# Threshold attention and a squared-ReLU layer on one core: the attention part's steps put in new orders, with values and turned weights in other PSUM banks

## The chip, the core and the metric

One NeuronCore of a Trainium2 chip runs the whole program. TensorE (PE) multiplies matrices and transposes; its weight loader is listed apart as PEld. VectorE (DVE), ScalarE (ACT) and GpSimd (POOL) do the elementwise work, and SyncE's queue (SP) issues nearly all DMAs. The metric is the device time of one execution in microseconds (us); the median of three runs stands for a kernel.

## What is computed

The reference runs attention in which only scores close to each row's maximum count, and feeds the result to a two-layer network:

```python
# q, k, v: (8, 8, 576, 64) float32; tau = 0.02
scores = q @ k.transpose(0, 1, 3, 2) / 8
thresh = scores.max(-1, keepdims=True) - tau
scores = where(scores >= thresh, scores, -1e9)
attn = exp(scores - scores.max(-1, keepdims=True))
attn = attn / (attn.sum(-1, keepdims=True) + 1e-9)
x = (attn @ v).transpose(0, 2, 1, 3).reshape(4608, 512)
out = maximum(x @ w_in, 0) ** 2 @ w_out      # w_in (512, 2048), w_out (2048, 512)
```

The two weight matrices arrive as 64-bit floats and are turned into 32-bit ones on the chip.

## The kernel before

The program has two parts, one after the other. The attention part comes first. The feed-forward part (`hidden_layer`, L837, and `output_layer`, L955) then does two layers of products with a seven-product scheme of sums and differences applied twice; its matmuls are L849 and L984. The change leaves it as it is.

**Units and periods.** A pair `i` is two heads of one batch entry, 32 in all. A unit is a block of 128 queries of both heads of a pair; every ninth unit (in two pairs) is made of the two rests of 64 queries. There are 144 units, handled two at a time (A and B) in 72 periods `p`. `period(p)` (L624) walks through a written list of step names and calls each; every engine executes its own steps in that order. Three lists exist: `PLAIN` (L599), `CONVERTING` (L602) for periods in which a chunk of the weights is also converted (`converts`, L590, periods 2 to 34), and `FIRSTS` (L606) for periods 0, 1 and 2.

**The steps** of one pair of units, in the order in which the data needs them:

- `T` turns (transposes) queries or keys of a later pair on PE into the middle of PSUM banks 1 and 4 (L399); `eT` evicts them with ACT (L406, L414) and issues the loads of the pair after that. `load_k` (L301) and `load_q` (L291) put these on SP's queue.
- `SA`: PE computes the main scores of A (banks 0 and 5) and the 64 last columns of A and B (the rims of banks 1 and 4); `SB`: the main scores of B (banks 2 and 3). Line L438.
- `topA0` to `topB1`: DVE copies a block of scores out of PSUM and takes its extreme (L456). `least`: POOL adds tau to it (L463). `pow`: ACT's exponential (L466). `mask`: DVE zeroes what is beyond the threshold and sums each row (L471).
- `over` (POOL, L478), `inv` (DVE, L481) and `spread` (POOL, L521) make the reciprocals of the row sums and write them out wide.
- `V`, `W`, `U`: PE turns the weights of 8, 2 (and the wide reciprocals) and 8 blocks (`half_turn`, L377, the transposes of L381); `eV`, `eW`, `eU`: ACT copies them to SBUF (`filled`, L523, the copies of L528).
- `PV`: PE multiplies by the values (`values`, L530, the matmuls of L537). `x`: DVE scales one head's result out of PSUM (L658), ACT copies the other's (L660). `xs`: POOL scales that one (L675) and SP stores both (L585).
- `c1` to `c6`: conversion of a chunk of weights: two passes on ACT (c1 L205, c2 L211), two on DVE (c4 L226, c5 L234), two on POOL (c3 L218, c6 L245). In the second half of the chunks a store follows c6 on SP's queue. `fetch` loads a chunk. `s1` and `sV` do one sum of weights on POOL, four on DVE (L122, L125). `id4`, `id14` keep PE busy in the first periods.

**PSUM before.** Eight banks of 512 columns. Six belong to the tile `sc`: banks 0 and 5 take A's main scores and later PV's result, banks 2 and 3 take B's main scores and later W (`middle`, L621), banks 1 and 4 the rims and T. The other two banks are the tile `pt`, one buffer, used in turn by U and by V. In period `p` the lists work on units of different ages: U, PV, x of the units of period `p - 2`, V, W, over, inv, spread of `p - 1`, scores to masks of `p`.

**Waits.** The framework makes an instruction wait for those whose data or buffers it needs. For the tile `sc`, `touch` (L356) sets this by bank: it adds a wait between two engines that touch the same bank and takes away one between different banks, except for the pairs of kinds in `MEET` (L354), which also meet in SBUF.

## Time and profile before

| what | us |
|---|---|
| median of three runs | 1290.56 |
| lowest and highest | 1289.38, 1292.22 |
| the profiled execution | 1292.2 |
| its span, first to last instruction | 1290.4 |
| busy in the span: PE, its loader | 1261.3, 1127.2 |
| busy in the span: DVE, POOL, ACT | 998.5, 897.4, 854.9 |
| mean granted clock of TensorE | 0.999 |

The span is the time between the first and the last instruction; some 1.8 us lie around it. Busy times of an engine are unions of its instructions' intervals, and an instruction of ACT or DVE is listed with its whole latency, so the next one often begins before the last has ended: what an engine can do is read from start to start. In a row of a timeline or of the chain stand the start, the duration, the engine, the line, the operation or the tile that it writes, and the count of instructions merged in it; in brackets the idle time ahead of it and what ended that. `sc` and `pt` are the PSUM tiles, `arena` is SBUF.

### The profile page before, as it was taken

How to read it: one execution, taken by the hardware profiler on the slowest of the kernel's cores; microseconds unless marked ns; L12 is line 12 of the kernel's file. 1: busy time of each engine (PE TensorE's matmuls, PEld its weight loads, DVE VectorE, ACT ScalarE, POOL GpSimd, SP SyncE). 2: the span in 40 equal slices, each digit the busy share in tenths (PEclk: the TensorE clock that was granted, in tenths of full speed). 3: DMA queues.
4: the chain of work that ended last, by engine and by line, in shares of the span. 5: the costliest groups of instructions: out<-in, count | busy, mean ns of one | idle time of the engine just before them, and what ended most of it. 6: DMA issues, size and time to landing. Idle time of an engine off the chain costs nothing.

```text
span 1290.4 us, 46352 instructions
## 1 busy us (share of the span) xinstructions
PE 1261.3 (98%) x18627; PEld 1127.2 (87%) x18627; DVE 998.5 (77%) x2433; ACT 854.9 (66%) x1536; POOL 897.4 (70%) x1094
## 2 busy tenths in 40 slices
PE   8999998999999999999999999999999999999998
PEld 6666666677777768999999999999999999999998
DVE  6999999899999997787788778777745654665463
ACT  6999999899999995756675667566523432343240
POOL 2565565555555557888898789768777867776775
PEclk9999999999999999999999999999999999999999
DMA  5555666544333422556655665589545314522411
GB/s 149 157 149 152 162 189 182 140 94 115 88 83 83 103 48 67 180 169 205 204 185 177 212 199 178 176 322 394 188 148 164 113 57 160 165 90 79 160 34 34
DMA packets 247032, 192.05 MB, mean 149 GB/s; under 512 B 97184, under 2 KB 195488, under 8 KB 246816
## 3 DMA queue, kind: packets, MB, share of 16 engines
q1 hardware_dynamic: 245360, 188.63, 48.7%
q8 instruction: 147, 2.41, 0.8%
q10 hardware_dynamic: 1456, 0.44, 0.1%
q14 instruction: 69, 0.57, 0.1%
HBM read 116.65 MB, written 72.35 MB: 146 GB/s over the span
## 4 chain that ended last, share of the span: by engine, by line
PE 64%; DMA 2%; DVE 1%; ACT 1%; issue 0%; POOL 0%; SPq 0%; ACTq 0%; DVEq 0%; POOLq 0%
PE ph L849 30%; PE po L984 29%; PE sc L537 2%; PE sc L438 2%; DMA wall<-w 1%; PE pt L381 1%; DMA g<-arena 0%; PE sc L381 0%; PE sc L399 0%; DVE arena L456 0%; ACT c L795 0%; ACT arena L528 0%; DVE arena L125 0%; DVE arena L122 0%; POOL arena L125 0%
## 5 line engine op out<-in xcount | busy, mean ns | idle before, releaser
L125 POOL TENSOR_TENSOR arena<-arena 128x512 f32<-128x512 f32 (+1 forms) x314 | 378.1, 1224 | 108.7 <-DVE arena L125 92.0
L984 PE MATMUL po<-wall,arena 128*128 128x128 f32 x3528 | 394.7, 275 | 1.4 <-ACT arena L761 1.4
L984 PEld LDWEIGHTS po<-wall,arena 128*128 128x128 f32 x3528 | 394.3, 192 | 1.8 <-ACT arena L761 1.8
L849 PE MATMUL ph<-arena,wall 128*128 128x128 f32 x3528 | 394.4, 275 | 0.5 <-DVE arena L658 0.5
L849 PEld LDWEIGHTS ph<-arena,wall 128*128 128x128 f32 x3528 | 394.1, 192 | 0.7 <-ACT arena L660 0.6
L125 DVE TENSOR_TENSOR arena<-ph,arena 128x512 f32<-128x512 f32 x378 | 256.1, 688 | 86.9 <-PE ph L849 62.6
L122 POOL TENSOR_TENSOR arena<-arena 128x128 f32<-128x128 f32 (+2 forms) x314 | 255.2, 814 | 54.5 <-DMA arena<-w 36.7
L125 DVE TENSOR_TENSOR arena<-po,arena 128x128 f32<-128x128 f32 x378 | 108.2, 289 | 168.4 <-PE po L984 164.3
L466 ACT ACTIVATE arena<-arena 128x576 f32<-128x576 f32 x288 | 224.3, 858 | 16.7 <-DVE arena L456 16.7
L471 DVE SCALAR_TENSOR_TENSOR arena<-arena 128x576 f32<-128x576 f32 x288 | 225.7, 812 | 0.4 <-POOL arena L463 0.3
L456 DVE TENSOR_SCALAR_CACHE_REDUCE arena<-sc 128x576 f32<-128x576 f32 x288 | 204.2, 750 | 18.0 <-ACT arena L528 6.8
L795 ACT COPY c<-arena 128x512 f32<-128x512 f32 (+1 forms) x303 | 173.5, 579 | 49.5 <-DVE arena L122 41.5
L537 PEld LDWEIGHTS sc<-arena 64*64 64x64 f32 x5760 | 144.8, 133 | 44.3 <-DVE arena L456 40.4
L122 DVE TENSOR_TENSOR arena<-arena,c 128x512 f32<-128x512 f32 (+1 forms) x267 | 174.6, 662 | 5.8 <-ACT c L795 4.0
L438 PE MATMUL sc<-arena 64*64 64x64 f32 (+1 forms) x2304 | 170.6, 417 | 0.3 <-DVE arena L658 0.2
L537 PE MATMUL sc<-arena 64*64 64x128 f32 (+1 forms) x5760 | 160.6, 262 | 9.9 <-DVE arena L456 7.8
L528 ACT COPY arena<-pt 128x1024 f32<-128x1024 f32 x144 | 157.4, 1093 | 3.6 <-PE pt L381 3.6
L761 ACT COPY arena<-po 128x128 f32<-128x128 f32 x63 | 16.6, 264 | 186.8 <-PE po L984 184.0
L381 PEld LDWEIGHTS pt<-ident,arena 64*128 64x128 f32 x2304 | 83.3, 139 | 42.7 <-ACT arena L528 35.3
L761 ACT COPY arena<-ph 128x512 f32<-128x512 f32 x63 | 36.6, 581 | 121.8 <-PE ph L849 121.2
L381 PE MATMUL pt<-ident,arena 64*128 64x64 f32 x2304 | 101.0, 228 | 3.7 <-ACT arena L528 3.5
L438 PEld LDWEIGHTS sc<-arena 64*64 64x64 f32 x2304 | 62.8, 133 | 47.0 <-issue 22.6
(51 smaller groups left out, 941.4 us busy)
## 6 DMA issues: line engine op xcount, KB each, us to landing
g<-arena SPq DMA_DIRECT2D x144, 256.0 KB, 2.8
arena<-g SPq DMA_DIRECT2D x144, 256.0 KB, 4.2
w<-arena SPq DMA_DIRECT2D x60, 256.0 KB, 2.5
wall<-w SPq DMA_DIRECT2D x49, 256.0 KB, 5.3
arena<-w SPq DMA_DIRECT2D x44, 256.0 KB, 3.1
arena<-in_v_dram SPq DMA_DIRECT2D x32, 288.0 KB, 3.6
out_dram<-arena SPq DMA_DIRECT2D x70, 128.0 KB, 2.5
arena<-in_q_dram SPq DMA_DIRECT2D x64, 128.0 KB, 3.8
```

What stands on the lines that cost most here:

```text
L122: e.tensor_tensor(out=out, in0=x, in1=y, op=ALU.subtract)
L125: e.tensor_tensor(out=out, in0=x, in1=y, op=ALU.add)
L381: made = nc.tensor.transpose(pt[:, r, ts(slot, HALF)], of[rows, :], ident[rows, rows])
L438: made = nc.tensor.matmul(sc[at, ds(to, count)], lhs, kT[rows, ds(at_k, count)], start=True, stop=True)
L456: made = nc.vector.tensor_scalar(out=s[:, j, :], in0=sc[:, ds(at, S)], scalar1=1.0, scalar2=None, op0=ALU.mult, op1=ALU.min, accum_out=nmx ...
L466: nc.scalar.activation(out=w[:, :, j, :], in_=of(j), func=AF.Exp, bias=nmx[:, j : j + 1], scale=-1.0)
L471: nc.vector.scalar_tensor_tensor(out=w[:, :, j, :], in0=of(j), scalar=thr[:, j : j + 1], in1=w[:, :, j, :], op0=ALU.is_le, op1=ALU.mult, a ...
L528: touch("weights", nc.scalar.copy(joined(to), whole(pt, 0, count)), at, 2 * BANK, m)
L537: made = nc.tensor.matmul(sc[ds(u * D, D), ds(5 * j * BANK + row, count)], loaded_v[i][rows, (c - (u != j)) % CH, :], wT[m][rows, ds(weigh ...
L795: nc.scalar.copy(c, y)
L849: nc.tensor.matmul(to[:, j, :], W_IN[m, k][:, ts(j, P)], of[k][:, m - 1, :], start=(not more and j == 0), stop=True, skip_group_check=True,)
L984: nc.tensor.matmul(to, g[:, j, :], w[:, j, :], start=(not more and j == 0), stop=(j == 3), skip_group_check=True)
```

## The change

- PV's result goes to the tile `pt`, which it shares with U. V moves to `middle` (banks 2 and 3), W to banks 0 and 5. W is evicted by two copies, one a bank. `MEET` loses two kinds of pairs that no longer meet in `sc`.
- All lists are new. A step name may carry a lag (`leastA@1`, `eV@2`): `period(p)` then does that step for the units of period `p - lag`. `LAGS` has the default lags. When the lists change from one period to the next, `due` sees that each step is done once for every period.
- In `PLAIN`, least, mask and one power of a period move to the start of the next; V's and W's evictions lag into the next period; T, U stand ahead of the scores, PV right behind them, W and V at the end.
- In `CONVERTING`, U moves one period earlier, between SA and SB; T moves from the start to behind W; c5 and c6 from the end to the start; c3 and c4 to the same period as c1.
- `converts` is true for one period more (2 to 35), and there is a list for period 3.
- `load_k` loads the last key rows of both heads by one DMA and not by two, and evictions of T go in the other order of banks.

```diff
-            queue.dma_start(out=rn[REST:P, ds(j * D, D)], in_=keys[:, CH - 1, :])
         queue = nc.sync if i else nc.scalar
-        queue.dma_start(
-            out=rn[0:REST, :].rearrange("p (j d) -> p j d", j=2),
-            in_=q[b, h : h + 2, MAIN:S, :].rearrange("j p d -> p j d"),
-        )
+        both = lambda rows: rn[rows, :].rearrange("p (j d) -> p j d", j=2)
+        last = k[b, h : h + 2, :, :].rearrange("j (p c) d -> p c j d", c=CH)[:, CH - 1, :, :]
+        nc.sync.dma_start(out=both(ds(REST, REST)), in_=last)
+        queue.dma_start(out=both(ds(0, REST)), in_=q[b, h : h + 2, MAIN:S, :].rearrange("j p d -> p j d"))
...
-    MEET = (("q scores", "turned q", (Q_RING,)), ("scores", "turned k", (K_RING,)), ("q scores", "turned k", (K_RING,)), ("values", "weights", (W_RING,)), ("x", "weights", (W_RING,)))
+    MEET = (("q scores", "turned q", (Q_RING,)), ("scores", "turned k", (K_RING,)), ("q scores", "turned k", (K_RING,)))
...
-                for r, n in ((0, half), (1, half + REST)):
+                for r, n in ((1, half + REST), (0, half)):
...
-                for r in range(2):
+                for r in (1, 0):
...
-        to = wT[m][:, ds(weight_at(first) * P, count * P)]
-        touch("weights", nc.scalar.copy(joined(to), whole(pt, 0, count)), at, 2 * BANK, m)
-
-    def values(m):
+        to = joined(wT[m][:, ds(weight_at(first) * P, count * P)])
+        if f == "W":
+            for r in (1, 0):
+                of = pt[r][:, ds(0, count * HALF)].rearrange("p (t q) -> p t q", q=HALF)
+                touch("weights", nc.scalar.copy(to[:, r, :, :], of), at[r], BANK, m)
+            return
+        of = pt[:, :, ds(0, count * HALF)].rearrange("p r (t q) -> p r t q", q=HALF)
+        touch("weights", nc.scalar.copy(to, of), at, 2 * BANK, m)
+
+    def values(m, to):
...
-                        made = nc.tensor.matmul(
-                            sc[ds(u * D, D), ds(5 * j * BANK + row, count)], loaded_v[i][rows, (c - (u != j)) % CH, :],
+                        nc.tensor.matmul(
+                            to[ds(u * D, D), j, ds(row, count)], loaded_v[i][rows, (c - (u != j)) % CH, :],
...
-        return is_wide and (has_chunk(p) or has_chunk(p - 1))
+        return is_wide and any(has_chunk(p - i) for i in range(3))
...
     PLAIN = """
-        fetch U SA topA1 over s1 topA0 SB topB1 inv sV eU powA1 V topB0 leastA spread PV powA0 maskA1 leastB maskA0 eV T powB1 x maskB1 powB0 xs maskB0 eT W eW
+        fetch leastA@1 eW@2 U leastB@1 maskA0@1 maskB0@1 maskA1@1 powB1@1 maskB1@1 eV@2 T SA topA0 over inv sV s1 eU eT xs@3 SB topA1 spread topB0 powA0 PV topB1 powA1 powB0 W x V
     """.split()
     CONVERTING = """
-        fetch c1 T SA topA1 c3 topA0 U eU powA1 SB topB0 over topB1 powA0 c4 powB0 PV eT inv leastA maskA1 x powB1 leastB spread V eV maskA0 W maskB0 c5 c6 eW maskB1 xs c2
+        fetch over SA c5 eV@2 c1 c6 topA1 U@1 topA0 leastA eU@1 powA1 inv SB xs@3 PV powA0 spread topB0 maskA1 W powB0 topB1 maskA0 T c3@0 c2 powB1 eW x c4@0 leastB maskB1 V eT maskB0
     """.split()

     FIRSTS = {
         0: """
-            SA SB id4 fetch topA1 topA0 powA1 leastA powA0 topB1 T id14 powB1 topB0 powB0 eT maskA0 leastB maskA1 maskB1 maskB0
+            fetch U@1 SA W spread topA1 SB topA0 powA1 eU@1 leastA topB0 powA0 topB1 powB1 maskA0 powB0 V eW leastB maskA1 id14 T x maskB1 eT PV xs@3 id4 maskB0 over eV@2 inv
         """.split(),
         1: """
-            SA topA1 SB topA0 id4 topB0 over inv powA1 V eV spread T powA0 topB1 eT W id4 leastA maskA1 leastB powB1 maskA0 maskB1 powB0 maskB0 fetch eW
+            fetch over SA topA1 id4 powA1 SB inv topA0 powA0 topB0 powB0 topB1 leastA spread leastB U@1 maskA1 W eW maskB0 eV@2 T powB1 eT PV eU@1 maskB1 maskA0 x xs@3 V
         """.split(),
         2: """
-            T SA fetch c2 U topA1 c3 over eU SB powA1 topA0 c4 powA0 c5 topB0 powB0 leastA topB1 eT maskA1 PV inv powB1 V leastB x spread maskA0 eV maskB1 maskB0 W eW xs c6 c1
+            fetch SA eV@2 over topA1 c5 c1 inv topA0 U@1 leastA c6 eU@1 powA1 SB PV powA0 spread topB0 W powB0 maskA1 xs@3 c2 topB1 maskA0 T c3@0 powB1 c4@0 leastB eW V maskB0 eT x maskB1
+        """.split(),
+        3: """
+            fetch c5 eV@2 c1 over SA U@1 topA1 c6 topA0 leastA xs@3 inv eU@1 SB topB0 spread PV powA1 topB1 W c2 powA0 maskA1 powB0 T c3@0 c4@0 leastB powB1 eW maskB0 eT x V maskB1 maskA0
         """.split(),
     }

+    LAGS = dict(
+        U=2, V=1, W=1, eU=2, eV=1, eW=1, PV=2, x=2, xs=2, over=1, inv=1, spread=1, c3=1, c4=1, c5=1, c6=1,
+    )
+    due, late = {}, {}
...
+    def turned_weights(f, m):
+
+        if not has(2 * m):
+            return
+        if f == "U":
+            late[f, m] = pt_pool.tile([P, 2, BANK], FP32, tag="pt", name="pt")
+            fill(m, f, [late[f, m][:, r, :] for r in range(2)])
+        elif f == "V":
+            late[f, m] = middle()
+            fill(m, f, [late[f, m][:, r, :] for r in range(2)], (2 * BANK, 3 * BANK))
+        else:
+            late[f, m] = [sc[:, ds(b * BANK, BANK)] for b in (0, 5)]
+            fill(m, f, late[f, m], (0, 5 * BANK))
+
+    def evict(f, m):
+
+        if has(2 * m):
+            filled(m, f, late.pop((f, m)), {"U": None, "V": 2 * BANK, "W": (0, 5 * BANK)}[f])
...
+    def values_of(m):
+
+        if has(2 * m):
+            late["PV", m] = pt_pool.tile([P, 2, BANK], FP32, tag="pt", name="px")
+            values(m, late["PV", m])
+
+    def given_out(m):
+
+        if not has(2 * m):
+            return
+        of = late.pop(("PV", m))
+        x = sb.tile([P, 2, P], FP32, tag="x", bufs=2, name="x")
+        one = nc.vector.tensor_tensor(out=x[:, 0, :], in0=of[:, 0, 0:P], in1=wT[m][:, ts(SCALE_AT, P)], op=ALU.mult)
+        other = nc.scalar.copy(x[:, 1, :], of[:, 1, 0:P])
+        tc.declare_no_dep(other.ins, one.ins, reason="other halves")
+        late["x", m] = x, wT.pop(m)
+        valued(m)
...
+    def period(p):
+
+        todo = []
+        for at, step in enumerate(FIRSTS.get(p) or (CONVERTING if converts(p) else PLAIN)):
+            name, _, lag = step.partition("@")
+            if name in in_order:
+                todo.append((p, at, in_order[name], p))
+                continue
+            lag = int(lag or LAGS.get(name, 0))
+            for q in range(due.get(name, 0), p - lag + 1):
+                todo.append((q + lag, at, steps[name], q))
+            due[name] = max(due.get(name, 0), p - lag + 1)
+        for _, _, step, q in sorted(todo, key=lambda t: t[0:2]):
+            step(q)
```

140 lines of the change are left out of this document (48 added, 92 removed).

## Prediction

> **What bounds it now.** I read the table by stages first (busy time in windows cut at the first score matmul of periods 0, 3, 36 and 71 and at the first matmul of the feed-forward part), then the chain that ended last, then the timelines of single periods. Columns of the table: window, its length, then busy time (instructions) of PE, PEld, DVE, ACT, POOL, the granted clock, DMA share and GB/s.
>
> ```profile
> 8.32:27.51 19.19, 17.11 (x295) 11.21 (x294) 16.49 (x48) 13.93 (x25) 4.50 (x10) 1.00 0.65 174
> 27.51:262.32 234.81, 218.93 (x5287) 154.96 (x5284) 228.26 (x659) 230.32 (x403) 140.03 (x231) 0.99 0.59 159
> 262.32:481.79 219.47, 218.38 (x5592) 158.01 (x5590) 211.07 (x631) 209.27 (x355) 121.47 (x210) 1.00 0.38 87
> 481.79:496.19 14.40, 11.96 (x364) 9.67 (x365) 13.32 (x33) 9.89 (x16) 5.38 (x11) 1.00 0.16 31
> 496.19:1290.41 794.22, 788.92 (x7056) 788.25 (x7056) 528.62 (x1062) 388.68 (x735) 625.36 (x628) 1.00 0.50 164
> ```
>
> The last row, 794.22 us, is the feed-forward part with PE and its loader full; the change doesn't touch it. What can move is the 487.9 us above it: 33 converting periods (7.12 us each), where ACT and DVE are both 97 to 98% busy and PE is not the bound, and 35 plain ones (6.27 us each), where PE has 1.1 us to spare in 219. In a plain period the chain is PE from end to end:
>
> ```profile
> 435.16 2.19 PE sc L537 x72
> 437.36 0.45 PE sc L399 x10
> 437.81 0.25 PE sc L381 x8
> 438.06 0.50 PE pt L381 x16
> 438.56 2.26 PE sc L438 x32
> 440.82 0.65 PE pt L381 x16
> ```
>
> That is PV, T, W, U, the scores SA and SB, and V: 6.30 us. The rows to look at are the 16 transposes: 0.50 behind other transposes, 0.65 behind scores. A change of matmul form costs about 0.15 in the piece behind it, and there are four a period (into T, into scores, into V, into PV).
>
> **Plain periods, part by part.** New PE order: U T | SA SB PV | W V, and on into U. V now stands behind W (0.50 for 0.65), W pays the form change that T paid (T: 0.45 less 0.14, W: 0.25 plus 0.14, nothing in sum), PV stands behind scores and not behind transposes; that saving has no row of its own, so 0 to 0.2, and I take 0.15 like the others. PE's work: 6.30 - 0.15 - 0.15 = 6.00 with ten T transposes (bounds 5.95 to 6.15), less with eight or none. PE falls to where DVE already is:
>
> ```profile
> 438.86 0.81 DVE L471 SCALAR_TENSOR_TENSOR arena<-arena 128x576 f32<-128x576 f32 x1
> 439.60 0.08 DVE L471 DVE_READ_ACCUMULATOR arena<-arena 128x1 f32 x1
> 439.95 0.76 DVE L456 TENSOR_SCALAR_CACHE_REDUCE arena<-sc 128x576 f32<-128x576 f32 x1 [0.28 <-ACT arena L528]
> ...
> 477.19 0.76 DVE L456 TENSOR_SCALAR_CACHE_REDUCE arena<-sc 128x576 f32<-128x576 f32 x1
> ...
> 483.18 0.76 DVE L456 TENSOR_SCALAR_CACHE_REDUCE arena<-sc 128x576 f32<-128x576 f32 x1
> ```
>
> From 477.19 to 483.18, the same step of two periods without a T, DVE never pauses: 5.99 us is its own period. At 439.95 it has waited 0.28, for PE's scores by the order of the steps (the row names ACT, whose copy it doesn't read). So of 6.27 at most 0.28 can go. A mask takes 0.74 (438.86 to 439.60), four are 2.96, and the other 3.03 are tops, inverse and x.
>
> The new order makes a ring of DVE and POOL that the old one did not have. The masks of a period run in the next one, ahead of its tops; leastA, which the first mask needs, stands on POOL behind over, s1, xs and spread, and over needs the last mask of the period before. The POOL rows:
>
> ```profile
> 439.77 0.23 POOL L478 TENSOR_SCALAR arena<-arena 128x4 f32<-128x4 f32 x1 [1.46 <-DVE arena L471]
> 440.08 1.28 POOL L122 TENSOR_TENSOR wall<-wall 128x512 f32<-128x512 f32 x1
> 441.50 0.29 POOL L463 TENSOR_SCALAR arena<-arena,tau_p 128x2 f32<-128x2 f32 x1
> 442.30 0.40 POOL L521 COPY arena<-arena 128x256 f32<-128x256 f32 x1 [0.51 <-DVE arena L481]
> 442.91 0.79 POOL L463 TENSOR_SCALAR arena<-arena,tau_p 128x2 f32<-128x2 f32 x1 [0.22 <-DMA arena<-in_k_dram]
> 444.20 0.46 POOL L675 TENSOR_TENSOR arena<-arena 128x128 f32<-128x128 f32 x1 [0.50 <-ACT arena L660]
> ```
>
> Last mask's end (439.60 + 0.08) to over 0.09, over to s1 0.31, s1 1.28, xs 0.46, spread 0.40, leastA 0.29: 2.83, and 3.1 with a gap like the one after over (0.08) at each hand-over. DVE's own work from the same point is 3.03 - 0.08 = 2.95. So the first mask comes 0 to 0.15 late. leastB comes right behind leastA and so beside the first mask; the second L463 row, which ran beside masks, took 0.79 against 0.29. The second mask (0.74 after the first) then waits about 0.1, or 0.3 (its own 0.29) if leastB only gets through when the mask ends. Together 5.99 to 6.45. I take 6.12: 0.05 for the late leastA and 0.1 for leastB (0.79 plus a hand-over, less 0.74, the nearest row).
>
> The Trainium skill, SBUF - State Buffer, section Who interferes with whom, says that a DVE instruction with two SBUF inputs contends with a GpSimd instruction that reads SBUF, and that the later one blocks. The mask has two such inputs, and 0.79 against 0.29 agrees; by that rule leastB would be held to the mask's end every period, the upper end of the last paragraph.
>
> PV's result now shares its buffer with U, and U must wait until x has been read by DVE and, behind powB0, by ACT. This ring: first top 0.75, the end of T's eviction 0.4, three powers 2.01 (row below), x and its hand-over 0.45, U 0.5, T 0.3, form change 0.15, SA to the first top 1.3: 5.9, hidden behind DVE's 5.99 and gone as cover from 0.1 on. ACT's own work (four powers 2.68, two wide copies 1.78, W 0.52, T 0.8, x 0.15, by the rows below) is 5.9 too. The first plain period inherits no U and no masks; I put it at 5.85. So plain: 5.85 + 34 x 6.12 = 213.9, **5.5 less**.
>
> **Converting periods.** ACT and DVE set them:
>
> ```profile
> 162.05 0.98 ACT L211 ACTIVATE arena<-arena 128x512 int32<-128x512 uint32 x1
> 162.64 0.95 ACT L205 ACTIVATE arena<-arena 128x512 f32<-128x512 f32 x1
> 163.23 1.27 ACT L528 COPY arena<-pt 128x1024 f32<-128x1024 f32 x1
> 164.12 2.38 ACT L466 ACTIVATE arena<-arena 128x576 f32<-128x576 f32 x3
> 166.13 0.96 ACT L414 COPY arena<-sc 128x256 f32<-128x256 f32 x2
> 166.70 0.60 ACT L406 ACTIVATE arena<-sc,qscale 128x64 f32<-128x64 f32 x1
> ```
>
> ACT is in line from start to start: c2 0.59, a 1024-wide copy 0.89, three powers 2.01. DVE's own period there is 6.9 (228.26 / 33 busy). Nothing of this work goes away. W's one eviction becomes two of half the width: the two key copies took 0.57 (166.13 to 166.70, of 256 and 320), so about 0.52 for the 0.48 of one, 0.04 more. And the order ties a ring: SA, U, eU, powA1, powA0, powB0, c2, powB1, eW, and SA again, because W now lies in SA's own banks and U stands between SA and SB.
>
> ```profile
> 160.72 1.32 PE L438 MATMUL sc<-arena 64*64 64x512 f32 x24
> 162.00 0.71 PE L381 MATMUL pt<-ident,arena 64*128 64x64 f32 x16
> ```
>
> SA to U 1.28, U 0.71, hand-over 0.1, eU 0.89, powers 2.01, c2 0.59, powB1 0.67, eW's first copy 0.26 and its second with the hand-over 0.45: 6.96, say 7.0. A period with a T or k eviction has ACT work of 7.0 to 7.1 (now 7.02 to 7.12). I take 7.08 for 31 periods, and 6.5 for the two that convert nothing but keep the order: 232.5, **2.3 less**. The gain is not in the order itself but in two places where the present order loses:
>
> ```profile
> 223.90 0.43 PE L399 MATMUL sc<-ident,arena 64*128 64x64 f32 x7 [0.36 <-DMA arena<-in_k_dram]
> 225.41 0.34 PE L399 MATMUL sc<-ident,arena 64*128 64x64 f32 x2 [1.08 <-DMA arena<-in_q_dram]
> ...
> 255.48 0.71 PE L381 MATMUL pt<-ident,arena 64*128 64x64 f32 x16 [1.35 <-ACT arena L528]
> ```
>
> In the first two T waits for its rows; the third is the seam to the plain order. Without these 2.8 us the present periods are (234.81 - 2.8) / 33 = 7.03. T moves from the period's start to behind PV; c6, whose store stands on SP's queue ahead of the loads, moves from the period's end to its start, so loads leave most of a period earlier against their T; two key DMAs become one. I count these losses gone, and nothing for fetch, c1 to c6 and the stores: they lie beside ACT's queue. If that cover is gone, a T late by a load costs 1 to 1.5 us each time.
>
> **Ends.** Start: DVE waits for T's form in banks 1 and 4 twice, as here:
>
> ```profile
> 12.33 0.76 DVE L456 TENSOR_SCALAR_CACHE_REDUCE arena<-sc 128x576 f32<-128x576 f32 x1 [0.50 <-PE sc L399]
> ...
> 489.64 2.06 DVE L122 TENSOR_TENSOR wall<-wall 128x512 f32<-128x512 f32 x3
> ```
>
> T now follows the tops in periods 0 and 1: **1.0 less** for two such waits. Tail, from the last SA: to the first top 1.45, tops and x 3.05, the masks held over 3.1, over and inverse 0.7, four sums of the last row's kind 2.7, x 0.4, U 0.6, eU 1.1, PV 2.7 (it is one with a rest block), x 0.5: 16.3 for the 14.40 of now, **1.9 more**. One POOL sum (1.28) moves into the feed-forward part; 0 to 1.3, taken as 0, since POOL has 169 us free there.
>
> Sum: -5.5 - 2.3 - 1.0 + 1.9 = -6.9. The profiled run took 1292.2 (span 1290.4 and 1.8 around it), so 1285.3; it lay 1.6 above the median of the three runs, so **1283.7** as a median.
>
> **Rivals.** (1) **Both rings close at their floors**: plain 5.99, converting 7.0: 209.5 and 230, with the ends' +0.9 in all -13.9: 1276.7. For it: DVE did run at 5.99. Against: two rings of POOL and ACT with no slack. (2) **ACT's ring in the converting periods is longer than its parts**: 0.08 more at each of four hand-overs makes 7.3, 31 x 0.22 = 6.8 back: 1290.5, no change. (3) **Slower**: leastB is held behind the first mask in every plain period and leastA is late too: 6.45 x 34 + 5.85 = 225.2, 5.7 more than now; with the other terms +4.3: 1294.9. Slower by over 0.2% it is from a plain period of 6.40 on. For it: 0.79 beside masks; against: leastB may get in before the mask, since the mask waits for leastA anyway.
>
> **How the numbers follow.** A measurement of this kernel can tell about 0.2% (2.6 us) from no change. Forecast 0.55, rival 1 0.15, rival 2 0.12, rival 3 0.18. Faster 0.70, same 0.12, slower 0.18. The likeliest case by itself spans 1279 to 1288 (plain 5.99 to 6.22); the range goes down to rival 1 and up to the foot of rival 3: 1275 to 1293.
>
> **What would show it.** Plain periods of 6.0 to 6.2 with DVE without gaps but one small one ahead of the first or second mask, released by POOL; the 16 transposes of V at 0.50; converting periods of 7.0 to 7.1 with no PE wait on loads; a tail of 16. Wrong if plain periods stay over 6.3, if PE waits for x ahead of U, or if SA waits on eW for more than 0.2.

## The result, and the profile after

The changed kernel took **1296.2 us** (median of 6, 1294.2 to 1296.7), the kernel before 1290.1 beside it: a ratio of 1.0043 with an interval of 1.003 to 1.0056. In a later set beside other runs of the kernel before the ratio was 1.0019 (1.0001 to 1.0036). It is 0.2 to 0.4% **slower**; the forecast was 1283.7, faster, and the time lies above the range's end of 1293.

This is the table by stages of the changed kernel's profile (window, its length, then busy time and instructions of PE, PEld, DVE, ACT, POOL, the granted clock, DMA share, GB/s), cut at the same places as the one in the prediction:

```profile
8.04:27.28 19.24, 16.71 (x301) 10.58 (x300) 16.89 (x48) 15.05 (x27) 5.26 (x11) 1.00 0.77 201
27.28:266.11 238.83, 215.27 (x5288) 147.91 (x5288) 233.92 (x662) 233.32 (x438) 150.03 (x229) 1.00 0.57 155
266.11:481.34 215.23, 213.69 (x5582) 158.30 (x5581) 209.91 (x625) 206.90 (x387) 118.41 (x209) 1.00 0.38 87
481.34:499.58 18.24, 13.65 (x367) 11.23 (x365) 14.59 (x35) 10.74 (x18) 6.00 (x11) 0.91 0.16 30
499.58:1294.82 795.24, 789.05 (x7056) 788.29 (x7056) 528.62 (x1062) 388.53 (x735) 626.63 (x629) 1.00 0.50 164
```

| stage | before, us | after, us | change | forecast |
|---|---|---|---|---|
| up to the first scores | 8.32 | 8.04 | -0.3 | 0 |
| periods 0 to 2 | 19.19 | 19.24 | 0 | -1.0 |
| converting, 33 periods | 234.81 | 238.83 | +4.0 | -2.3 |
| plain, 35 periods | 219.47 | 215.23 | -4.2 | -5.5 |
| last scores to feed-forward | 14.40 | 18.24 | +3.8 | +1.9 |
| feed-forward | 794.22 | 795.24 | +1.0 | 0 |

The changes add up to the spans' 4.4. The plain periods gained nearly what was worked out. The converting stage and the tail took it back, and more. One caution on the column "before": two later profiles of that kernel have 232.2 and 231.4 in the converting stage, so its first profile, on which the forecast rests, carried some 3 us there that are not usual. Against these two the converting stage lost 7 us and not 4.

**Plain periods.** 6.27 us became 6.16 (34 periods from period 37 on). DVE's and POOL's rows around one hand-over in the timeline (L466 is the mask, L458 least) show what is left above DVE's own time:

```profile
436.76 0.91 POOL L458 TENSOR_SCALAR arena<-arena,tau_p 128x2 f32<-128x2 f32 x1
436.78 0.81 DVE L466 SCALAR_TENSOR_TENSOR arena<-arena 128x576 f32<-128x576 f32 x1
437.52 0.08 DVE L466 DVE_READ_ACCUMULATOR arena<-arena 128x1 f32 x1
437.70 0.82 DVE L466 SCALAR_TENSOR_TENSOR arena<-arena 128x576 f32<-128x576 f32 x1
```

leastB starts beside the first mask and ends at 437.67, just behind the mask's end (437.60); the second mask, of B, starts at 437.70, 0.10 late. All later steps follow without a pause.

**Converting periods.** ACT's rows of one period, from eV to the next eV, in the timeline:

```profile
165.55 1.04 ACT L529 COPY arena<-sc 128x1024 f32<-128x1024 f32 x1
166.44 0.72 ACT L205 ACTIVATE arena<-arena 128x512 f32<-128x512 f32 x1
167.03 1.04 ACT L529 COPY arena<-pt 128x1024 f32<-128x1024 f32 x1
167.93 2.14 ACT L461 ACTIVATE arena<-arena 128x576 f32<-128x576 f32 x3
169.93 0.74 ACT L211 ACTIVATE arena<-arena 128x512 int32<-128x512 uint32 x1
170.52 0.81 ACT L461 ACTIVATE arena<-arena 128x576 f32<-128x576 f32 x1
171.19 0.68 ACT L526 COPY arena<-sc 128x256 f32<-128x256 f32 x2
171.71 0.33 ACT L672 COPY arena<-px 128x128 f32<-128x128 f32 x1
171.86 0.77 ACT L409 COPY arena<-sc 128x320 f32<-128x320 f32 x2
172.44 0.40 ACT L401 ACTIVATE arena<-sc,qscale 128x64 f32<-128x64 f32 x1
172.65 1.10 ACT L529 COPY arena<-sc 128x1024 f32<-128x1024 f32 x1
```

No row has idle time ahead of it: 7.10 us from eV to eV is ACT's own work. PE waits in such a period, at SA for eW (next fence), but it waits for an engine that is not idle.

```profile
164.83 1.37 PE L433 MATMUL sc<-arena 64*64 64x512 f32 x24 [0.38 <-ACT arena L526]
```

The prediction named a wait of SA for eW of more than 0.2 as a sign of being wrong. It came, but by itself it doesn't tell a ring that sets the period from slack. Beside the periods around a stop of PE (below) and one wait of 0.3 in period 4, ACT runs dry only in the three places where no T is evicted, and then for U:

```profile
115.96 0.71 ACT L205 ACTIVATE arena<-arena 128x512 f32<-128x512 f32 x1
117.22 1.01 ACT L529 COPY arena<-pt 128x1024 f32<-128x1024 f32 x1 [0.55 <-PE pt L380]
```

Of the 31 periods that convert, 28 took 7.11 on average (forecast 7.08). Three single ones (4, 6 and 29) took 7.57, 9.14 and 7.77, and the two that convert nothing (34 and 35) 6.79 and 8.45 where 6.5 each was forecast. The 9.14 is a stop of PE in the middle of 16 transposes; the bracket gives the idle time and "issue", which is to say that nothing the profile shows was waited for:

```profile
55.28 0.54 PE L380 MATMUL sc<-ident,arena 64*128 64x64 f32 x11
57.94 0.34 PE L380 MATMUL sc<-ident,arena 64*128 64x64 f32 x5 [2.12 <-issue]
```

The 8.45 is the seam to the plain order. There T stands ahead of SA, and it writes where eT of the period before, the last step of ACT in the converting list, still reads; DVE then has nothing to do:

```profile
264.62 0.86 ACT L401 ACTIVATE arena<-sc,qscale 128x256 f32<-128x256 f32 x2
...
265.54 0.59 PE L394 MATMUL sc<-ident,arena 64*128 64x64 f32 x10 [1.30 <-ACT arena L401]
...
267.50 0.76 DVE L451 TENSOR_SCALAR_CACHE_REDUCE arena<-sc 128x576 f32<-128x576 f32 x1 [1.77 <-issue]
```

**Tail.** PE stands still until eU, last in ACT's queue, is done. PV then takes 3.77 for 72 matmuls, which took 2.19 in the fence of the prediction (435.16):

```profile
489.76 3.77 PE L538 MATMUL px<-arena 64*64 64x128 f32 x72 [2.23 <-ACT arena L529]
...
496.61 2.33 PE L538 MATMUL px<-arena 64*64 64x128 f32 x108 [1.65 <-ACT arena L529]
```

The reason why it took longer stands in the clock's column (the 0.54 and 0.60) of the table by windows:

```profile
488.00:490.00 2.00, 0.24 (x8) 0.25 (x12) 1.65 (x7) 1.70 (x2) 0.23 (x1) 1.00 0.01 1
490.00:492.00 2.00, 2.00 (x48) 2.00 (x44) 1.93 (x4) 0.00 (x0) 1.20 (x2) 0.54 0.11 22
492.00:494.00 2.00, 2.00 (x47) 1.67 (x42) 1.57 (x4) 0.27 (x1) 0.08 (x1) 0.60 0.27 52
```

DVE is not what the tail waits for. It stands idle ahead of its last step, x of the last pair, until PV is done:

```profile
499.14 0.29 DVE L671 TENSOR_TENSOR arena<-px,arena 128x128 f32<-128x128 f32 x1 [2.48 <-issue]
```

### The profile page after: what moved, and what is told of

It is laid out like the page before. It is cut to its first block, busy times and chain, and to the rows that moved or that the text cites. A ratio compares the mean times of both kernels' runs of the same rounds, so it can differ in the third digit from the quotient of the medians.

```text
span 1294.8 us, 46358 instructions
## 1 busy us (share of the span) xinstructions
PE 1254.4 (97%) x18623; PEld 1121.4 (87%) x18623; DVE 1004.6 (78%) x2433; ACT 857.5 (66%) x1608; POOL 907.0 (70%) x1094
## 4 chain that ended last, share of the span: by engine, by line
PE 67%; ACT 14%; issue 5%; DVE 5%; DMA 4%; POOL 2%; SPq 2%; ACTq 0%; DVEq 0%; POOLq 0%
PE ph L865 30%; PE po L1000 27%; ACT arena L529 4%; ACT arena L461 4%; PE sc L433 4%; PE px L538 3%; DVE arena L451 2%; DVE arena L466 2%; PE sc L380 1%; ACT arena L526 1%; PE pt L380 1%; POOL arena L458 1%; ACT arena L401 1%; SPq L310 1%; DMA arena<-g 1%
## 5 line engine op out<-in xcount | busy, mean ns | idle before, releaser
L466 DVE SCALAR_TENSOR_TENSOR arena<-arena 128x576 f32<-128x576 f32 x288 | 229.0, 824 | 5.5 <-POOL arena L681 0.3
L461 ACT ACTIVATE arena<-arena 128x576 f32<-128x576 f32 x288 | 211.8, 798 | 9.0 <-DVE arena L451 8.9
L451 DVE TENSOR_SCALAR_CACHE_REDUCE arena<-sc 128x576 f32<-128x576 f32 x288 | 207.0, 746 | 7.9 <-PE sc L433 4.5
L538 PEld LDWEIGHTS px<-arena 64*64 64x64 f32 x5760 | 146.1, 134 | 66.7 <-ACT arena L529 65.8
L538 PE MATMUL px<-arena 64*64 64x128 f32 (+1 forms) x5760 | 162.1, 263 | 11.4 <-ACT arena L529 10.1
L473 POOL TENSOR_SCALAR arena<-arena 128x4 f32<-128x4 f32 x72 | 28.7, 399 | 161.1 <-DVE arena L466 157.2
L433 PEld LDWEIGHTS sc<-arena 64*64 64x64 f32 x2304 | 56.6, 132 | 71.1 <-issue 23.7
L458 POOL TENSOR_SCALAR arena<-arena,tau_p 128x2 f32<-128x2 f32 x144 | 80.0, 556 | 39.5 <-DVE arena L451 27.1
L845 ACT ACTIVATE arena<-arena 128x512 f32<-128x512 f32 x144 | 90.8, 631 | 4.6
```

The lines of the kernel that those rows point to most:

```text
L433: made = nc.tensor.matmul(sc[at, ds(to, count)], lhs, kT[rows, ds(at_k, count)], start=True, stop=True)
L451: made = nc.vector.tensor_scalar(out=s[:, j, :], in0=sc[:, ds(at, S)], scalar1=1.0, scalar2=None, op0=ALU.mult, op1=ALU.min, accum_out=nmx ...
L458: nc.gpsimd.tensor_scalar(out=thr, in0=nmx, scalar1=tau_p[:, :], scalar2=None, op0=ALU.add)
L461: nc.scalar.activation(out=w[:, :, j, :], in_=of(j), func=AF.Exp, bias=nmx[:, j : j + 1], scale=-1.0)
L466: nc.vector.scalar_tensor_tensor(out=w[:, :, j, :], in0=of(j), scalar=thr[:, j : j + 1], in1=w[:, :, j, :], op0=ALU.is_le, op1=ALU.mult, a ...
L538: nc.tensor.matmul(to[ds(u * D, D), j, ds(row, count)], loaded_v[i][rows, (c - (u != j)) % CH, :], wT[m][rows, ds(weight_at(2 * c + u) * P ...
```

## The experiments

My theory after this profile was that W, now in the banks of SA's scores, ties ACT and PE into a ring that sets the converting periods, and that the tail lost to a halved clock. The rivals were: ACT's own work sets the periods; single stalls and the seam cost what was lost; the new PSUM places rather than the orders are at fault. Ratios are to the kernel before, run beside each; the changed kernel's own are 1.0043 and 1.0019.

**One step off the supposed ring.**

```diff
-... T c3@0 c2 powB1 eW x c4@0 leastB ...      (CONVERTING)
+... T c3@0 powB1 eW c2 x c4@0 leastB ...
```

> Only the order of the converting periods is changed: the conversion step c2 (0.59 us on ACT) is issued behind eW and not ahead of powB1. Theory: the 31 converting periods of 7.1 to 7.2 us are a ring through ACT and PE (SA, U, eU, powA1, powA0, powB0, c2, powB1, eW, SA), because W now lies in the banks of SA's scores; with c2 off the ring PE no longer waits for eW ahead of SA, and a period falls to ACT's own work of about 7.0: 0.1 to 0.15 x 31, 3 to 5 us less than the changed kernel's 1296.2, so 1291.5 to 1293. Rival (the periods are ACT's own work, and the ring only shows a wait that costs nothing): the wait moves to eU, periods stay 7.12 to 7.16, 1295.5 to 1297. Rival (the loss is stalls of single periods, such as the 9.14 us of period 6): typical periods as before this edit, the long ones still there.

Ratio **1.0128** (1.011 to 1.0146), 1308.0 us: some 12 slower than the changed kernel, which neither theory nor rivals had. Periods are 7.5 to 7.6 with a T of keys or queries, 6.87 without. ACT's rows:

```profile
159.15 2.16 ACT L461 ACTIVATE arena<-arena 128x576 f32<-128x576 f32 x3
161.66 0.78 ACT L461 ACTIVATE arena<-arena 128x576 f32<-128x576 f32 x1 [0.34 <-DVE arena L451]
162.34 0.62 ACT L526 COPY arena<-sc 128x256 f32<-128x256 f32 x2
162.85 0.70 ACT L211 ACTIVATE arena<-arena 128x512 int32<-128x512 uint32 x1
```

powB1 needs DVE's fourth top, which comes 0.34 after the third power's end; c2 had filled just that gap. And eT, which SA's last columns need, still stands behind c2. A step that "sits on a chain" was the filler of a wait. That ACT idles here in every period, and the period grows, speaks for ACT as the bound.

**U at the head of the period.**

```diff
-fetch over SA c5 eV@2 c1 c6 topA1 U@1 topA0 ...      (CONVERTING)
+fetch over U@1 SA c5 eV@2 c1 c6 topA1 topA0 ...
```

> Only the order of the converting periods is changed: U is issued at the head of the period, ahead of SA and not behind it, so that eU need not follow SA. Theory of the ring: SA to U (1.28 us) falls out of it, no wait of PE on eW of more than 0.1 is left, and the periods fall to ACT's work: 7.0 or a little under, 31 x 0.15 = 4 to 5 us less than the changed kernel: 1291 to 1292.5. Rival (ACT's own work): 7.12 to 7.16 as in the changed kernel, 1295.5 to 1297. A second way to go wrong: SA starts 0.7 later behind U, and DVE's first tops with it; if DVE (6.9 us a period) then becomes late, the periods are 7.2 to 7.4 and the time 1298 to 1303.

Ratio **1.0562** (1.054 to 1.0584), 66 to 70 us slower, periods of 8.5 to 9.9. I had overlooked what U reads:

```profile
164.79 0.28 PE L380 MATMUL pt<-ident,arena 64*128 64x64 f32 x2 [0.55 <-ACT arena L672]
166.07 0.71 PE L380 MATMUL pt<-ident,arena 64*128 64x64 f32 x14 [1.00 <-DVE arena L466]
```

U turns the weights of the period before, whose last mask is DVE's last step; ahead of SA it makes masks, U, SA and tops one chain with nothing of DVE's beside it. So this run doesn't tell the ring from ACT's work. It shows why U stands behind SA.

**Masks in the order A A B B.**

```diff
-... maskA0@1 maskB0@1 maskA1@1 powB1@1 maskB1@1 eV@2 T SA ...      (PLAIN)
+... maskA0@1 maskA1@1 maskB0@1 powB1@1 maskB1@1 eV@2 T SA ...
```

> Only the order of the plain periods is changed: both masks of A come ahead of those of B, so that the second mask no longer needs leastB, which POOL makes beside the first. Theory: the 0.10 to 0.18 us of DVE's idle time ahead of the second mask is all that is left above DVE's own 5.99; plain periods fall from 6.15 to 6.0 to 6.05, 34 x 0.1 to 0.15: 3.5 to 5 us less than the changed kernel, 1291 to 1293. Rival (leastA is late as well, or PE's and ACT's ring through x, U and eU is as long): the idle time moves to the first mask or to the tops, periods 6.12 to 6.18, 1295 to 1297.

Ratio **1.0014** (1.0001 to 1.0027), 1292.9 us: 2.4 to 3.4 less than the changed kernel. Plain periods fell from 6.16 to 6.08 and the stage from 215.23 to 212.55. DVE's rows:

```profile
435.45 0.81 DVE L466 SCALAR_TENSOR_TENSOR arena<-arena 128x576 f32<-128x576 f32 x1
436.19 0.08 DVE L466 DVE_READ_ACCUMULATOR arena<-arena 128x1 f32 x1
436.19 0.81 DVE L466 SCALAR_TENSOR_TENSOR arena<-arena 128x576 f32<-128x576 f32 x1
...
438.72 0.76 DVE L451 TENSOR_SCALAR_CACHE_REDUCE arena<-sc 128x576 f32<-128x576 f32 x1 [0.19 <-ACT arena L401]
```

The second mask now starts when the first ends. Part of the gain goes to a new wait: the masks end earlier, and the second top waits. In this profile the tail took 19.70, 1.5 more, with the clock halved twice in it and not once. Half theory, half rival.

**PE kept busy in the tail.** Sixteen transposes of the identity ahead of PV in period 72.

```diff
+    in_order["idT"] = lambda p: p == NU // 2 and keep_busy(16, sc[:, ds(BANK, P)])
-... topB0 powA0 PV topB1 powA1 powB0 W x V      (PLAIN)
+... topB0 powA0 idT PV topB1 powA1 powB0 W x V
```

> One step is added in the period behind the last scores alone: 16 transposes of the identity, which write to a bank that nobody reads, ahead of PV. Theory: in the tail PE stood still for 2.23 us for eU, the granted clock then was 0.5 for 3.4 us, and PV took 3.77 for the 2.20 that it takes elsewhere; with PE at work during the wait the clock stays at 1.0, PV takes 2.2 to 2.4, and the tail from the last SA to the feed-forward part falls from 18.24 to about 16.7: 1294.7. Rival (the 0.5 is not an answer to the idle time, or PV is slow for another reason): 18.2 as before, or the transposes themselves run at half speed and PV still takes over 3: 1296 to 1297.

Ratio 1.004 (1.0026 to 1.0054), no different from the changed kernel. The mechanism is there: the clock stays at 1.00, and

```profile
487.44 1.04 ACT L529 COPY arena<-pt 128x1024 f32<-128x1024 f32 x1
487.62 1.97 PE L1053 MATMUL sc<-ident 128*128 128x128 f32 x16 [1.31 <-ACT arena L529]
...
489.51 2.20 PE L538 MATMUL px<-arena 64*64 64x128 f32 x72
```

PV takes 2.20, 1.57 less. But the tail is 17.61, only 0.6 shorter: the sixteen transposes outlast the wait that they fill. eU (the ACT row) ends at 488.48 and PV starts 1.03 behind it, where it started 0.06 behind it in the changed kernel.

**A period of its own for the seam.**

```diff
-        return is_wide and any(has_chunk(p - i) for i in range(3))
+        return is_wide and any(has_chunk(p - i) for i in range(2))
+        35: fetch leastA@1 eW@2 U leastB@1 maskA0@1 maskB0@1 maskA1@1 powB1@1 maskB1@1 eV@2 SA topA0 over
+            inv s1 eU xs@3 SB topA1 spread topB0 powA0 PV topB1 T powA1 powB0 W eT x V      (FIRSTS)
```

> The converting order ends one period earlier (after period 34), and period 35 has a list of its own, the plain order with T behind SB and eT behind W. In the changed kernel the last two periods before the plain stage took 6.79 and 8.45 us: the second because T(36) stands ahead of SA in the plain order and waited 1.30 us for eT(35) at the end of the converting one, with DVE idle for 1.77. Theory (a seam between the two orders, a term the forecast had at zero): the two periods become 6.2 to 6.6 each, 2 to 2.8 us less in that stage, 1293.4 to 1294.2 in all against the changed kernel's 1296.2. Rival (the 1.30 us is slack, ACT and DVE have the same work anyway): the time moves into the neighbouring periods and the sum of periods 34 to 37 stays within 0.5 us, 1296.

Ratio 1.0031 (1.0016 to 1.0046). Periods 34 and 35 took 7.28 and 7.38, 14.66 for the 15.24 of the changed kernel's first profile: 0.6 less, not 2 to 2.8. PE's 1.30 was mostly slack of two orders that hand over work of different ages; the price of this seam is 0.6 as far as this list can take it away.

**The old list on the new places.** The converting list of the kernel before, all else as changed.

> The list of the converting periods is that of the kernel before, while values and turned weights keep their new PSUM places; lists of the first four periods, the plain one and all else are the changed kernel's. It tells places from orders. Theory 1 (ACT's and DVE's work sets the period, and neither place nor order matters much): typical periods of 7.0 to 7.1, 1293 to 1297. Theory 2 (W in the banks of SA's scores needs the new order): SA must wait for eW, which stands at the end of the old list, so SA, four tops, c4, two masks, W and eW are one chain: 1.45 + 2.7 + 0.6 + 0.1 + 0.73 + 0.2 + 0.73 + 0.25 + 0.5 + hand-overs is 7.4 to 7.6 a period, 31 x 0.35 to 0.45 is 11 to 14 us more than the changed kernel: 1307 to 1310.

Ratio **1.0316** (1.0292 to 1.034), periods of 8.13 to 8.22, longer than theory 2 had. PE's and DVE's rows at the start of a period (L526 is eW):

```profile
161.41 1.32 PE L433 MATMUL sc<-arena 64*64 64x512 f32 x24 [1.72 <-ACT arena L526]
...
162.87 0.76 DVE L451 TENSOR_SCALAR_CACHE_REDUCE arena<-sc 128x576 f32<-128x576 f32 x1 [1.05 <-ACT arena L205]
```

The places alone cost 1 us a period, because W holds SA's banks until eW at the list's end; the new order takes that back. Place and order belong together, and together they bring the converting periods to ACT's work, where the old pair already was.

**A new tail.** PV of the last two pairs writes to banks 1 and 4, and period 72 has a list.

```diff
+        72: fetch leastA@1 U eW@2 leastB@1 maskA0@1 maskB0@1 maskA1@1 powB1@1 maskB1@1 eV@2 eU over
+            inv spread PV xs@3 V x U@1 W sV eV@1 eW@1 eU@1      (FIRSTS)
```

> Only the end of the attention part is changed: PV of the last two unit pairs writes to the banks of the scores that have no more scores to hold, so that it need not follow eU, and period 72 has a list of its own, with V and U of the last pair right behind PV of the one before, and eV, eW, eU behind them. Theory (the tail's waits, with the half clock that came after one, are what it lost): PE's longest wait falls from 2.23 to about 1.2, the granted clock stays 1.0, PV(70) takes 2.2 and not 3.77, and the tail falls from 18.24 to 14 to 14.5 us: 1292 to 1292.5 against 1296.2. Rival (the masks held over and POOL's inverse and spread set the tail): W of the last pair still comes at 492 or later, the tail is 16 to 17, 1294 to 1295.

In this list spread overwrites a row that xs still has to read, so half of one pair's output gets a wrong scale: its steps and times can be read, but it is no kernel to use. Ratio 1.0034 (1.0016 to 1.0052). The clock stayed at 1.00 and the tail fell to 16.78, to the rival's value but not for its reason. DVE's rows:

```profile
495.12 2.28 DVE L122 TENSOR_TENSOR wall<-wall 128x512 f32<-128x512 f32 x3
497.31 0.28 DVE L682 TENSOR_TENSOR arena<-sc,arena 128x128 f32<-128x128 f32 x1
```

ACT had its half of x at 495.71; DVE took the other 1.6 later, behind its sums.

**All three together, with this tail.**

> The masks' order A A B B in the plain periods, the list of its own for the period between the two orders, and the new tail, together: candidate for a kernel that beats both. If the three gains are independent: 1296.2 - 3 (masks) - 2.3 (seam) - 4 (tail) = 1287, under the 1290.1 of the kernel before, a ratio of 0.997 to 0.998. If the tail's gain is swallowed by the masks, which now end later (leastB and the last mask): 1289 to 1290, no difference from before.

Ratio 1.0006 (0.9992 to 1.002), 1292.2 us: no different from the kernel before. The output has the same fault as that of the tail alone.

**The tail once more.**

```diff
-... eU over inv spread PV xs@3 V x U@1 W sV eV@1 eW@1 eU@1
+... eU over inv xs@3 spread PV V x U@1 W sV eV@1 eW@1 eU@1 PV@1 x@1
```

> The new tail once more, with two steps placed otherwise: x of the pair before is scaled ahead of spread on POOL (spread overwrites the row that it needs, so the first form gave half of one pair's output a wrong scale), and PV and x of the last pair stand in period 72's list, so that DVE takes x ahead of its second set of four sums. Theory (the last x waited behind those sums: they ran from 494.4 to 497.4 while PV had ended at 495.6): the tail falls from 16.78 to about 15, 3 us less than the changed kernel's 18.24, so 1293. Rival (the feed-forward part's first products need those sums): its first matmul starts early but it stops for them, the tail and the feed-forward part together gain nothing over the first form, 1294 to 1296.

xs now stands ahead of spread, which mends the scale. The tail is 15.34, so the sums were what held it, as the theory had it. But the rival holds too. The feed-forward part starts earlier and then stops for those sums at its 41st matmul:

```profile
504.58 1.61 PE L876 MATMUL ph<-arena,wall 128*128 128x128 f32 x12 [1.41 <-DVE arena L125]
```

The tail and the feed-forward part together take 811.5 (15.34 and 796.15); with the first form they took 811.3 (16.78 and 794.52). The ratio, 1.0016 (0.9999 to 1.0034), can't be told from that of the changed kernel in the same set.

**The changed kernel again.**

> The changed kernel itself, unchanged, for a second profile and more times beside the others. In its first profile PE stopped for 2.12 us in the middle of 16 transposes at 57.9 with nothing waited for, 2.4 us after an instruction transfer that came 9.2 us after the one before it, and period 6 took 9.14. The profile of the kernel with the first new tail, whose program is the same up to period 72, took 7.16 there. Theory (the stall is one of chance in when the instruction transfers come, not of the order): the second profile differs from the first by up to 2 us in periods 6 and 29 and the times spread over 3 us or more. Rival (it belongs to this program): period 6 again over 8.5.

Period 6 took 7.21 for 9.14, but period 29 8.59 for 7.77, with 1.44 of a stop in it; 11 times spread from 1293.8 to 1298.5. Theory right. The kernel with the first new tail, the same program up to period 72, ran V's transposes of period 6 in one piece:

```profile
55.32 0.77 PE L380 MATMUL sc<-ident,arena 64*128 64x64 f32 x16
```

So whether a stop comes and how long it is differ from one execution to the next. But all ten profiles with the new converting list had 1.3 to 4.2 us of stops over 0.3, in period 6, in period 29 or in both, and the kernel before, U first and the old list had 0 to 0.35.

**A version ahead of both**: masks A A B B, the seam's period, the second tail.

> The masks' order A A B B, the period of its own between the two orders and the corrected tail together: candidate to beat both. The first form of this with the faulty tail had a ratio of 1.0006 to the kernel before; the corrected tail should take another 1.5 us: 1290.5 for a before of 1292, a ratio of 0.999, within what can be told from no change; under 0.998 only if the converting periods' stalls are also fewer than in the changed kernel.

1289.6 us (1288.4 to 1291.5, 11 runs), ratio **0.998** (0.9964 to 0.9996): 0.2% under the kernel before, which is as little as can be told from no change, and 0.4% under the changed one of the same set. Its profile still has a stop of 1.99 in period 6. Its stages:

```profile
27.43:264.63 237.20, 214.68 (x5284) 148.04 (x5285) 232.79 (x659) 231.45 (x436) 150.16 (x229) 1.00 0.58 156
264.63:476.75 212.12, 211.06 (x5584) 157.00 (x5581) 209.35 (x629) 208.02 (x389) 115.16 (x210) 1.00 0.39 89
476.75:491.91 15.16, 12.04 (x367) 9.80 (x365) 11.52 (x32) 10.77 (x18) 5.69 (x11) 1.00 0.19 36
```

Against the kernel before, the plain stage (219.47) brings 7.4; the converting stage (234.81) takes 2.4 of it, or 5.4 by the two later profiles of that kernel, and the tail 0.8. Here the feed-forward part doesn't stop for the sums; it took 794.8.

**The kernel before, twice more, and the changed program shifted.** The shift is 32 more transposes of the identity in period 0 (`id14 id14 id14 id4` for `id14`).

> The kernel before itself, for a second profile. Ten profiles with the new converting list have 1.3 to 4.2 us of stops of PE over 0.3 us with nothing waited for; the one profile of the kernel before has none, nor have U first and the old list on the new places more than 0.35. Theory (the stops came with the new list): again under 0.5 us. Rival (chance, one profile was lucky): 1 us or more.

> The changed kernel with 32 more transposes of the identity in period 0, which move every later instruction of PE by 64 places against the 256 of a 16 KB transfer of instructions, a quarter of one. The stops of the changed kernel stood at two places, in periods 6 and 29. Theory (they hang on where the program is cut into transfers): they come 1 to 2 us from their places within the period, in another step, or vanish. Rival (they hang on what else goes on in periods 6 and 29, loads above all): they stay in the same steps. The start is up to 3 us longer.

> The kernel before once more, a third profile, for the same question: theory under 0.5 us of stops, rival 1 us or more.

The kernel before: 0.4 and 0 us of stops, in single executions of 1288.9 and 1293.3. The shifted program took 1297.1, with 22.76 in periods 0 to 2 for 19.24. No stop of PE over 0.3 with "issue" stands in its converting stage, and its periods 6 and 7 took 7.15 and 7.07. But its period 29 took 7.94, and there the stop is, in another step: SA took 2.37, where it took 1.37 in that period in the second profile of the changed kernel, and PE's loader stood idle in it:

```profile
216.25 2.37 PE L433 MATMUL sc<-arena 64*64 64x512 f32 x24 [0.30 <-ACT arena L526]
...
217.31 0.63 PEld L433 LDWEIGHTS sc<-arena 64*64 64x64 f32 x12 [0.88 <-issue]
```

In the second profile of the changed kernel the stop of that period cuts U into 10 and 6 transposes. Counted from the start of the program it is the same place. Here are the windows up to the stop, of the second profile and then of the shifted program; the loader's column ends at 4550 in both:

```profile
0.00:218.10 218.10, 195.96 (x4549) 134.38 (x4550) 204.62 (x581) 204.33 (x383) 127.91 (x201) 0.99 0.61 163
0.00:217.30 217.30, 196.28 (x4549) 135.25 (x4550) 202.43 (x574) 203.11 (x382) 126.82 (x199) 1.00 0.60 159
```

So the place of a stop goes by the count of PE's instructions and not by the step, as the theory had it: of the two stops one moved and one didn't come. What brings them is open. A loader's stop of over 0.7 without anything waited for stands in all eleven profiles with the new converting list, the shifted one included, and in none of the five with another list (the kernel before three times, U first, the old list). The shift doesn't separate what the order does from how the program is cut into transfers.

The shifted program has 237.06 in the converting stage, of it 221.8 in the 31 periods that convert, some 0.8 of that in period 29. The kernel before took 217.4 and 216.7 for these in its new profiles.

## Why the prediction was wrong

**Right: the plain periods.** PE fell to DVE, DVE runs without pauses but one ahead of the second mask, and the price of leastB behind the first mask is 0.10, as taken; 6.16 for 6.12. Rival 3, a full 0.3 of leastB more, did not come. The stage gave 4.2 of 5.5. The first plain period, put at 5.85, took 5.91; the rest of the 1.3 is in the 34 others, 0.04 each, two longer ones (6.58 and 6.36) included.

**Failed: the converting periods, "2.3 less", with "I count these losses gone".** I put the stage at 232.5, and it took 238.8. Of the 6.3 between them, 3.2 are three long periods (4, 6 and 29), 2.2 are the seam, put at nothing, and 0.9 are the other 28 periods. Against the kernel before, three parts of this step failed.

The 2.8 us of losses that were to go were those of one profile. T's waits on its loads (and the halved clock that followed them, at 226.8 in that profile) are gone in the changed kernel, as forecast; but the kernel before mostly doesn't have them either: 217.4 and 216.7 us for 31 periods, 7.00 each, where the forecast's profile had 220.0. The seam stayed: 8.54 to 8.70 in the kernel before, 8.45 after. It stood in my own quoted rows (1.35 at 255.48), and I took it away without asking what the new lists do where they meet.

ACT's work grew by more than the 0.04 a period that I gave it. Summed over the ACT rows of the 31 periods (start to next start, idle time taken off) it is 216.7 before (mean of the two later profiles) and 219.3 in the shifted program: 0.08 a period. W's copies make 1.2 of these 2.6 us (62 of 0.258 for 31 of 0.478), c1 and c2 1.6 (0.62 each for 0.59; no run tells why, but with c2 behind eW that step took 0.585); the rest, longer small copies and shorter powers, nearly cancels. So my 7.08 for a period was near what ACT needs (7.07), but it is more than before, not less.

And ACT now has 2.7 us of idle time in these periods of the shifted program, 0.77 of it behind the stop, for 0 to 0.4 before. The ring of 6.96 is real, but it is a floor and not the bound: in a period with a T ACT has 7.1 of work and the ring doesn't show; in one without, the kernel before went through in 6.3 to 6.7, and now ACT waits 0.44 to 0.55 for U and the period is 6.9 to 7.0. I had priced the ring against ACT's mean and not against its short periods.

Together 221.8 for 217.0, some **5 us more**, about 0.8 of it the stop in period 29 (in the first two profiles, 223.6 for 220.0, some 2 of it the stop at 57.94). My first theory after the result, that the ring sets all these periods, fell with c2: its steps fill ACT's waits. Rival 2's 7.3 did not come.

**Failed: the tail's term, +1.9.** I added DVE's and POOL's work after the last scores, and PV at the speed of a running PE: 16.3. It took 18.24, and 1.57 of the 1.94 between them is PV: PE's idle 2.23 us ahead of it were missing from the sum, and behind them the clock was halved and PV took 3.77 for 2.20. The path was another one, too. DVE has 2.48 us of slack ahead of the last x; the tail goes through ACT's evictions and PE's PV, twice. With the clock kept it was 17.61, 0.97 of it the transposes that kept it. The sums do stand ahead of the last x in the first new tail; with x ahead of them, and V and U of the last pair turned earlier, the tail was 15.34.

**Missed: the start.** The two waits of DVE were to bring 1.0; the three periods took 19.24 for 19.19. The waits went, and periods 0 and 1 took 0.46 less (12.19 for 12.65), but period 2, which has a new list as well, took 7.05 for 6.54.

**The feed-forward part** was given nothing, rightly as far as can be told: the same program took 794.0 to 796.1 in the profiles of this study, whatever the attention part was, and 796.2 in the one where it stops for the sums.

leastB, recorded 0.02 ahead of the mask, ended 0.07 behind it (0.91 us beside the mask, 0.29 alone), and the mask kept its 0.74. The price was a hand-over and not leastB's 0.29 on top; why is not shown. The Trainium skill, SBUF - State Buffer, section Who interferes with whom, says that a DVE instruction with two SBUF inputs contends with a GpSimd instruction that reads SBUF, and that the order of issue decides which of the two blocks. The 0.91 agrees with the first; the second can't be told here, since the one that was held is recorded as the first by 0.02.

## What to carry to other kernels

Where an engine is idle nowhere, no order makes its stage shorter: count its work in both orders, price a new ring against the shortest periods and not the mean, and give the seams and the drain terms of their own. Follow the drain along the engine that is waited for, and count what a step takes behind a wait. A loss seen once in one profile is not a loss to be won back; look whether a second profile has it. When a step is moved "off the chain", look at what its old place was filling.

## What the runs showed of the hardware

**The clock.** In the changed kernel's tail PE was idle for 2.23 us with little work around it (0.24 of 2.00 in the window 488 to 490), and the records then grant 0.5 for 3.41 us. Eight profiles have that tail (the changed kernel's two, c2 late, U first, masks, seam, old list, shifted), with a wait of 2.21 to 2.24. In seven of them such a stretch starts within 1.2 us of the wait's end, in the eighth, the old list's, only 5.5 us behind it, at the next waits. The five with a wait of 1.3 there (transposes, both new tails, the two versions with all three edits) have none, though two of them wait 2.07 and 1.95 ahead of the feed-forward part. The kernel before waits 1.59 in its tail and has a stretch in one of three profiles, with a tail of 16.06 for 14.40. With U first, where PE waits in every period, there were 23 such stretches in the attention part and the mean clock was 0.97. So the length of a wait alone doesn't tell, but some 2 us can be enough. The Trainium skill, TensorE: Matmul & The Clock Gate, section What's actually happening, says that the gate falls to half after about 3.4 us of idle. Here a wait of 2.2 us was followed by it in seven profiles of eight, and one of 1.59 in one of three.

**Instruction transfers.** Each stop of PE of over 1 us with "issue" in its bracket had a 16 KB transfer on the queue of instructions that started 2.2 to 2.7 us ahead of its end. By the records these transfers start some 258 of PE's instructions apart in the changed kernel (the median; nine of ten lie between 167 and 361), and those ahead of such stops 399 to 498 after the one before. Ahead of the shifted program's stop the transfer came at 286, started 4.0 us ahead of the stop's end and took 2.34, where the median is 1.05. With the program shifted by 64 instructions the stop of period 29 stayed at the same count, 4550 weight loads. The Trainium skill, Runtime: NRT & Kernel Launch, section Instruction fetch mechanics, says that code comes in 16 KiB blocks of 256 instructions and that crossing one is mostly hidden. The spacing agrees, and at all but one or two of some 85 blocks no stop is seen. What makes these late, no run here tells.
